# A second expert by half products in seven pairs of token tiles, with a fused sum and ReLU

## The chip, the cores and the metric

The kernel runs on one core of one Trainium2 chip. The metric is the time of one execution on the device, in microseconds. Three runs of the kernel before gave 377.02, 377.45 and 377.55 us; the median is 377.45. The profiled execution took 377.47 us, and the span from its first to its last instruction is 375.8 us. TensorE had its full clock throughout.

## The reference

Two layers follow each other. The first is attention over 4 batches, 8 heads, 768 positions of 64 values. Heads 0, 2 and 6 ("retrieval heads") see every earlier position; the other five see the first 4 positions ("sinks") and a window of the last 64. The second is a mixture of four experts, of which every token uses all four:

```python
a = softmax(where(mask, q @ k.T / 8, -1e9))
x = (a @ v) as 3072 tokens x 512
p = domain_probs / (domain_probs.sum(-1, keepdims=True) + 1e-9)
for e in range(4):
    h = maximum(x @ w1[e], 0.0)        # 512 -> 1024
    out += p[:, e:e + 1] * (h @ w2[e]) # 1024 -> 512
```

As p is not negative, it may be multiplied into x ahead of the first layer of an expert instead of into its result; the kernel does so for all but the first four token tiles.

## The kernel before, in words

**Tiles and stages.** The tokens are 24 tiles of 128. Attention works on eight units of three tiles (half a batch each). The first four tiles go through the experts plainly (`plain_steps`). The other twenty go two by two, as ten pairs (`pair_steps`, here counted from 0). A pair has two layers. In layer 1 each expert's hidden values are computed into `hA`, which is cut into blocks: `A11` and `A21` (the first half of the hidden values, for the first and the second tile), `A12` and `A22` (the second half), and a fifth. In layer 2 all four experts are multiplied by `w2` at once.

**Half products.** A product of 2 x 2 blocks is computed with seven block products instead of eight, after Strassen and Winograd, at the price of sums of blocks. Layer 2 does this in every pair: `second_sum`, `third_sum` and `fourth_sum` build S2 to S4 out of S1 (`first_sum`), and seven products (`product`, line 1290) accumulate in two PSUM banks x and y, in the order x y x y x y x. Between them ScalarE copies a bank to `s` (`keep`) and VectorE adds bank and copy into the output `o` (`add`, line 1313): after the second product out of y, after the fifth out of x, after the sixth out of y. In layer 1 expert 3 (`EW[0]`) is done so in every pair, and expert 2 (`EW[1]`) in the last `LAST = 3` pairs (`two(nt0)`); the other experts use `plain_layer1` (line 1154: eight matmuls of 256 columns a step). `winograd_layer1` has seven steps of eight matmuls of 128 columns (line 1183). They alternate between two banks of `pO`, with one bank of `pA` for the second step; each is followed by a copy on ScalarE (line 1193), or by a sum on VectorE out of PSUM (line 1199) with a ReLU in place behind it (line 1205), or, the last, by a ReLU on ScalarE.

**What VectorE prepares.** `scale_inputs(nt0, e)` (line 1112) multiplies the tokens of a pair by expert e's probabilities. `scaled_sums(e)` (line 1126 and two differences at 967) builds the block sums of an expert's inputs, and `first_weight_sums(e)` those of its `w1`, once. The sums for expert 2 are computed in the sixth and seventh pairs, into room that attention no longer needs (`room_for_more_sums`).

**The order.** All engines' instructions are in an order written out by hand; every engine works through its own queue in that order. A pair's layer 1 is a list of rows (`order`, lines 1250 and 1266): each names the steps to take from the generators n (plain), a and b (half products of experts 3 and 2) and then an operation, mostly for VectorE. A pair also prepares the next one: during and after its fifth and sixth product the inputs of experts 3 and 0 (and 2, if the next pair has two experts by half products: `ahead`) are scaled, and `scaled_sums` of expert 3 follows. Attention is put between these steps by a plan: each step reports its TensorE time times a share (0.5 in layer 1, 1.57 in layer 2), and while this sum is ahead of the plan of the current attention unit, one attention step is put in. An attention step is some scores (line 659), an exponent on ScalarE (677), a mask on VectorE (681), values (713, 785) and a normalisation (803, 808, 813 or 738 to 742); a unit begins by moving keys (273, 289).

**Keys and sinks.** The retrieval keys have two buffers `kR[0]` and `kR[1]`, by the parity of the batch; the values of the sinks that batches 1 to 3 need lie in `v_sinks`. POOL sets one key buffer to zero at line 1441, after the first attention unit, ahead of the loads of a later one. SP's queue carries the load of a pair's probabilities (`load_probs`, line 1089), the output's stores (1320) and the attention's transposes by DMA (262, 747).

Of the kernel before, what the change touches and what calls it, by code (L numbers as in the profile page):

```python
# [9 lines left out]

# [1 line left out]
FP16 = mybir.dt.float16  # L12
# [6 lines left out]
def kernel(  # L19
# [92 lines left out]

    EW = (E - 1, E - 2)
    KH, FN = DMP // 2, F // 2
    t1sb = pers.tile([P, 3, KH, FN], FP16, name="t1sb")
    hA = pers.tile([P, 5 * KT * P], FP16, name="hA")
    kR = []
    vR = []
    for i in range(2):
        kR.append(pers.tile([P, NCH, NR, 3, P], FP16, name=f"kR{i}"))  # L120
        vR.append(pers.tile([P, S // P, NR, D + 2], FP16, name=f"vR{i}"))
    kSf = pers.tile([P, NT * NSH * P], FP16, name="kS")
    vSf = pers.tile([P, NT * NSH * P], FP16, name="vS")

    kS = kSf.rearrange("p (c t s x) -> p c t s x", c=NCH, t=TC, s=NSH)
    vS = vSf.rearrange("p (c t s x) -> p c t s x", c=NCH, t=TC, s=NSH)

    def windows(x):

# [27 lines left out]


    kT = pers.tile([P, HP, P + CH], FP16, name="kT")
    v_sinks = pers.tile([NS, 1, NSH * P], FP16, name="v_sinks")  # L160

# [5 lines left out]
    def half(u):  # L167
        return slice(u * D, (u + 1) * D)
# [7 lines left out]

    def key_tile(b, c, h, t):

        i = b % 2
        if RETR[h]:  # L180
            return kR[i][:, t // 3, RH.index(h), t % 3, :]
# [88 lines left out]
    def keys_to_rows(b, c):  # L270

        for n, hps in ((slice(0, 2), slice(0, 2)), (slice(2, 3), slice(3, 4))):
            nc.vector.tensor_copy(
                out=kR[b % 2][half(0), c, n, :, :].rearrange("p n t x -> p n (t x)"),
                in_=kT[half(0), hps, P : P + CH],
            )

# [84 lines left out]
    def zero(eng, t):  # L362
        fill(eng, t.rearrange("p a b x -> p (a b x)"), 0.0)
# [53 lines left out]
    make_identity(nc, ident32)  # L417
    one_values(nc.vector, 0)
    load_v(0, 0, [0])
    zero(nc.vector, kR[0][:, 0, :, :, :])  # L420
    zero(nc.vector, kS[:, 0, :, :, :])
    nc.vector.tensor_copy(out=ident16, in_=ident32)

# [67 lines left out]
    load_v(0, 0, [2, 1, 3, 4, 6, 5, 7])  # L491
    load_w1(0, 0, F)
    load_w2(0)
    zero(gp, kR[0][:, 1, :, :, :])
# [44 lines left out]
    def attention(b, c):  # L539
# [8 lines left out]
        def transposes(hp):  # L548
            for x, is_k in ((q32 if first else qt16, 0), (k32 if first else k16, 1)):
                if first or hp > 1:  # L550
                    ps = bank()
                else:
                    ps = pV.tile([P, 512], FP32, name="pV", bufs=2)
                for j in range(3):
                    o = ps[:, j * P : (j + 1) * P]
                    if first:
                        nc.tensor.transpose(o, x[:, j, 2 * hp : 2 * hp + 2, :], ident32)
                        continue
                    for u in range(2):
# [12 lines left out]
                for u in range(2):  # L572
                    h = 2 * hp + u
                    r = slice(u * D, (u + 1) * D)
                    if RETR[h]:
                        nc.vector.tensor_copy(  # L576
                            out=rows_in_order(
                                kR[i][r, c, RH.index(h), :, :].rearrange(
                                    "r t x -> r (t x)"
                                )  # L580
                            ),
                            in_=cols(ps[r, :]),
                        )
                        continue
                    n = SH.index(h)
                    x_in, x_out = ps[r, 0:CH], kS[r, c, :, n, R0:P]
                    if first:
                        x_in = x_in.rearrange("r (t x) -> r t x", x=TK)
                    else:
                        x_in = x_in.rearrange("r (j t p) -> r j t p", j=3, t=TC)  # L590
                        x_out = x_out.rearrange("r t (p j) -> r j t p", j=3)
                    nc.vector.tensor_copy(out=x_out, in_=x_in)
                    sinks = kS[r, c, :, n, 0:NS]
                    if c == 0:
                        src = ps[r, 0:NS]
# [354 lines left out]

    hA16 = hA
    blocks = hA.rearrange("p (b k x) -> p b k x", b=5, k=KT)
    A11, A21, A12, A22, S1 = (blocks[:, n, :, :] for n in range(5))
    S2, S3, S4 = A11, A21, A12

    def whole_b(k, n, e, ft):
        return w2sb[:, e * FTP + k * HT + ft, n * HN : (n + 1) * HN]
# [20 lines left out]
        c = e * DMP + j * KH  # L978
        return w1sb[:, c : c + KH, k * FN : (k + 1) * FN]

    t1 = {(EW[0], n): t1sb[:, n, :, :] for n in range(3)}
# [10 lines left out]
    def room_for_more_sums():  # L992

        x = kR[0].rearrange("p c n t x -> p (c n t x)")
        y = att.tile([P, KH * FN], FP16, name="t1", tag="k_rows", bufs=1)
        for n in range(3):
            z = x[:, n * KH * FN : (n + 1) * KH * FN] if n < 2 else y
            t1[EW[1], n] = z.rearrange("p (c f) -> p c f", c=KH)
        x = att.tile([P, DMP * PC], FP16, name="xs1", tag="q16", bufs=1)
        own_room[EW[1]] = x.rearrange("p (c x) -> p c x", c=DMP)  # L1000

    own_room = {}

    def last_weight_sum(e):

# [126 lines left out]
    def first_sum(e, n=1):  # L1132
        k = slice(e * HT, (e + n) * HT)
        nc.vector.tensor_tensor(
            out=S1[:, k, :], in0=A21[:, k, :], in1=A22[:, k, :], op=ALU.add
        )


    PSHARE = 1.57

    LAST = 3

    def two(nt0):
        return nt0 >= pairs[-LAST]
# [1 line left out]
    def pair_steps(nt0, nxt):  # L1146
# [29 lines left out]
        def winograd_layer1(e, x, y):  # L1176
# [18 lines left out]
            def block(n):  # L1195
                return blocks[:, n, e * HT : (e + 1) * HT, :]

            def add(n, ps, b):
                nc.vector.tensor_tensor(  # L1199
                    out=block(b),  # L1200
                    in0=ps.rearrange("p (f x) -> p f x", f=HT),
                    in1=kept[n].rearrange("p (f x) -> p f x", f=HT),
                    op=ALU.add,
                )
                nc.vector.tensor_scalar(
                    out=block(b), in0=block(b), scalar1=0.0, scalar2=None, op0=ALU.max
                )

            def t(n):
# [29 lines left out]

        a, b = (winograd_layer1(e, *y) for e, y in zip(EW, (banks, banks[::-1])))  # L1240

        more, last_more = [], None
        if nt0 == pairs[-LAST - 2]:
            room_for_more_sums()
            more = first_weight_sums(EW[1])
        elif nt0 == pairs[-LAST - 1]:
            last_more = first_weight_sums(EW[1])[3]
        if not two(nt0):
            n = itertools.chain(*(plain_layer1(e) for e in range(E - 1)))
            order = (  # L1250
# [8 lines left out]
                ((n, a), lambda: first_sum(0, 2)),  # L1259
                ((n,), None),  # L1260
                ((n, n), lambda: first_sum(2, 2)),
                ((), lambda: scale_inputs(nxt, 1) if two(nxt) else None),
            )
        else:
            n = itertools.chain(plain_layer1(0), plain_layer1(1))
            order = (
                ((a, a, n), None),
                ((a, a, n), lambda: load_probs(nxt) if nxt else None),
                ((a, a, n), None),
                ((n,), lambda: scaled_sums(EW[1])),  # L1270
                ((a, b, n), None),
                ((b, b, n), lambda: first_sum(0)),
# [61 lines left out]

        last = nxt is None
        ahead = nxt and two(nxt)
        half = KT // 2 * mm_ns(HN), PSHARE
        yield from product(x, A11, b(0, 0), True)
        keep(0, x)
# [207 lines left out]
```

The softmax here doesn't subtract the row's maximum and nothing guards it: scores larger than these inputs give would overflow.

## Time and profile before

| | |
|---|---|
| median of three runs | 377.45 us |
| span of the profiled execution | 375.8 us |
| TensorE busy | 367.5 us (98%), 4128 matmuls |
| VectorE busy | 282.7 us (75%) |
| ScalarE busy | 227.8 us (61%) |
| plain layer 1, line 1154 | 864 matmuls of 256 columns |
| half products of layer 1, line 1183 | 728 matmuls of 128 columns |
| sums out of PSUM, line 1199 | 39, 26 of them at a mean of 687 ns |
| ReLUs in place, line 1205 | 39, mean 298 ns |
| scalings, line 1112, 1024 elements | 28, mean 1216 ns |

A matmul's duration in the trace includes its way through the array, and matmuls overlap; what one costs in a stream is the distance from its start to the next one's. "DVE" is VectorE, "ACT" ScalarE, "PE" TensorE and "PEld" its loading of weights. In a timeline a line is: start, duration, engine, line of the kernel, operation, what it writes and reads, shape, count of merged instructions, and in brackets the idle time before it and what ended it. VectorE's durations also overlap a little: for its pace, too, look at the starts. The ten pairs begin at about 88.1, 118.6, 149.3, 178.0, 209.5, 238.3, 267.8, 296.3, 321.7 and 347.2 us of the span; attention's last matmuls are in pair 6.

### The profile page before, as it was taken

The page shows a single profiled execution, that of the slowest core. Times are in us where ns is not written, and L with a number is a line of the kernel's source. Part 1 is how long each engine was busy: PE and PEld are TensorE (multiplying, and loading weights), DVE is VectorE, ACT ScalarE, POOL GpSimd, SP SyncE. Part 2 cuts the span into 40 slices and gives each one's busy share as a digit, 9 for nine tenths or more (in the row PEclk, how much of TensorE's full clock was granted, in tenths as well). Part 3 has the DMA queues.
Part 4 walks back from the last instruction along what each step waited for, and adds up shares of the span by engine and source line. Part 5 has one row for each costly group of instructions (what it writes and reads, how often), then busy time and mean ns, then how long its engine had stood idle before and what let it go on. Part 6 is the DMA issues. An engine that isn't in the chain of part 4 may idle for free.

```text
span 375.8 us, 10137 instructions
## 1 busy us (share of the span) xinstructions
PE 367.5 (98%) x4128; PEld 310.2 (83%) x4128; DVE 282.7 (75%) x620; ACT 227.8 (61%) x475; POOL 113.7 (30%) x155
## 2 busy tenths in 40 slices
PE   8889999999999999999999999999999999999996
PEld 4745466668998988999989898998899998999996
DVE  7774768697888679878758858967778868769572
ACT  3863478547785785765676955784777361450630
POOL 8934573882058038115601650320000000000000
PEclk9999999999999999999999999999999999999999
DMA  9999999999699599977904991951220300300101
GB/s 164 155 201 206 196 187 191 181 207 105 97 109 144 106 96 120 152 116 58 207 10 59 170 157 21 127 127 14 69 72 2 107 9 0 114 2 6 54 2 56
DMA packets 124771, 39.24 MB, mean 104 GB/s; under 512 B 113728, under 2 KB 118404, under 8 KB 124724
## 3 DMA queue, kind: packets, MB, share of 16 engines
q0 software_dynamic: 86848, 19.01, 59.1%
q1 hardware_dynamic: 36276, 19.18, 21.9%
q8 instruction: 32, 0.52, 0.6%
q10 hardware_dynamic: 1600, 0.39, 0.5%
q14 instruction: 15, 0.12, 0.1%
HBM read 44.89 MB, written 6.34 MB: 136 GB/s over the span
## 4 chain that ended last, share of the span: by engine, by line
PE 87%; DMA 7%; POOL 3%; DVE 2%; issue 0%; POOLq 0%
PE pO L1290 31%; PE pA L1154 25%; PE pO L1183 9%; DMA w2sb<-in_moe_w_dram 7%; PE pO L1048 6%; PE pA L659 5%; PE pA L1027 5%; PE pV L713 2%; PE pV L785 2%; PE pA L1183 2%; POOL vS L309 1%; POOL vR L303 1%; DVE xs L1112 1%; PE pA L1380 0%; POOL early L453 0%
## 5 line engine op out<-in xcount | busy, mean ns | idle before, releaser
L1290 PEld LDWEIGHTS <-hA 128*128 128x128 f16 x1104 | 104.9, 98 | 12.2
L1154 PE MATMUL pA<-xs,w1sb 128*128 128x256 f16 x864 | 109.3, 272 | 0.0
L1154 PEld LDWEIGHTS <-w1sb 128*128 128x128 f16 x864 | 80.7, 98 | 8.5
L1163 ACT ACTIVATE hA<-pA 128x512 f16<-128x512 f32 x108 | 64.4, 598 | 35.1 <-PE pA L1154 32.9
L1290 PE MATMUL pO<-w2sb,hA 128*128 128x256 f16 x640 | 76.7, 272 | 0.0
L677 ACT ACTIVATE es<-pA 128x384 f16<-128x384 f32 (+2 forms) x122 | 59.2, 511 | 27.1 <-PE pA L659 23.3
L305 POOL DMA_DIRECT2D vS<-in_v_dram x30 | 29.6, 989 | 111.7 <-PE pV L785 110.5
L1290 PE MATMUL pO<-tsb,hA 128*128 128x256 f16 x464 | 56.7, 272 | 0.0
L1112 DVE TENSOR_TENSOR xs<-xT,pB 128x1024 f16<-128x1024 f16 (+1 forms) x52 | 49.4, 969 | 1.2 <-DMA out_dram<-o 1.2
L967 DVE TENSOR_TENSOR hA<-hA 128x1024 f16<-128x1024 f16 x60 | 39.6, 684 | 0.4
L1040 ACT ACTIVATE hA<-pA 128x384 f16<-128x384 f32 (+1 forms) x64 | 22.2, 385 | 19.8 <-PE pA L1027 19.6
L1027 PE MATMUL pA<-xT,w1sb 128*128 128x384 f16 (+1 forms) x256 | 30.9, 273 | 1.3 <-DVE xT L766 0.8
L1048 PE MATMUL pO<-w2sb,hA 128*128 128x512 f16 x128 | 30.7, 379 | 0.3 <-DMA w2sb<-in_moe_w_dram 0.3
L1310 ACT COPY s<-pO 128x256 f32<-128x256 f32 x31 | 11.5, 372 | 27.7 <-PE pO L1290 21.9
L1027 PEld LDWEIGHTS <-w1sb 128*128 128x128 f16 x256 | 19.3, 98 | 10.2 <-issue 1.9
L808 DVE TENSOR_TENSOR xT<-pV,rc 64x384 f16<-64x384 f32 x37 | 20.5, 555 | 9.1 <-ACT rc L813 6.6
L1183 PEld LDWEIGHTS <-w1sb 128*128 128x128 f16 x416 | 26.3, 98 | 1.1 <-issue 0.2
L803 ACT ACTIVATE rc<-pV,eps 64x384 f32<-64x384 f32 x37 | 21.3, 576 | 6.5 <-PE pV L785 5.9
L1199 DVE TENSOR_TENSOR hA<-pO,s 128x512 f16<-128x512 f32 x26 | 17.9, 687 | 9.3 <-PE pO L1183 6.7
L681 DVE TENSOR_TENSOR es<-es,mS 128x384 f16<-128x384 f16 (+1 forms) x40 | 13.7, 343 | 13.4 <-ACT es L677 13.4
L659 PE MATMUL pA<-qT,kR 128*128 128x384 f16 (+2 forms) x120 | 22.9, 278 | 0.6 <-DVE kR L576 0.6
L1193 ACT COPY s<-pO 128x512 f32<-128x512 f32 x39 | 22.5, 585 | 1.4 <-PE pO L1183 1.2
(144 smaller groups left out, 498.2 us busy)
## 6 DMA issues: line engine op xcount, KB each, us to landing
pB<-p_rows SPq DMA_DIRECT2D x10, 512.0 KB
out_dram<-o SPq DMA_DIRECT2D x19, 256.0 KB
w1sb<-in_moe_w_dram POOLq DMA_DIRECT2D x8, 512.0 KB, 9.3
w2sb<-in_moe_w_dram POOLq DMA_DIRECT2D x4, 1024.0 KB, 12.5
vS<-in_v_dram POOLq DMA_DIRECT2D x30, 112.0 KB, 4.2
k_rows<-in_k_dram POOLq DMA_DIRECT2D x18, 128.0 KB, 5.6
q<-in_q_dram POOLq DMA_DIRECT2D x18, 128.0 KB, 6.4
vR<-in_v_dram POOLq DMA_DIRECT2D x24, 48.0 KB, 5.8
```

What stands on the lines that cost most here:

```text
L305: gp.dma_start(out=t[:, :, own_v(h)], in_=windows_of(v, b, h, c))
L659: nc.tensor.matmul(out=ps[:, o : o + nq], lhsT=key_tile(b, c, h, t), rhs=qTs[b, c][:, hp, q0 : q0 + nq], start=(n == 0 or not first), stop ...
L677: nc.scalar.activation(out=es[:, 0:cols], in_=ps[:, 0:cols], func=AF.Exp, scale=SC)
L967: nc.vector.tensor_tensor(out=out, in0=a, in1=b, op=ALU.subtract)
L1027: nc.tensor.matmul(out=pss[ft][:, 0:cols_n], lhsT=w1sb[:, e * DMP + ct, ft * P : (ft + 1) * P], rhs=x[:, ct, :], start=(n == 0), stop=(n = ...
L1048: nc.tensor.matmul(out=ps_o, lhsT=hs[:, ft, j * P : (j + 1) * P], rhs=w2sb[:, e * FTP + ft, :], start=(ft == 0), stop=(ft == FTP - 1),)
L1112: nc.vector.tensor_tensor(out=o, in0=xin, in1=pb.to_broadcast([P, DMP, n, P]), op=ALU.mult)
L1154: nc.tensor.matmul(out=ps[:, f * PC : (f + 1) * PC], lhsT=w1sb[:, e * DMP + ct, (f0 + f) * P : (f0 + f + 1) * P], rhs=xs[:, ct, :], start= ...
L1163: nc.scalar.activation(out=blocks[:, b0 : b0 + 2, k0 : k0 + 2, :].rearrange("p t f x -> p f t x"), in_=ps.rearrange("p (f t x) -> p f t x" ...
L1183: nc.tensor.matmul(out=ps[:, f * P : (f + 1) * P], lhsT=w[:, ct, f * P : (f + 1) * P], rhs=a[:, ct, :], start=(first and f == 0 and ct == ...
L1193: nc.scalar.copy(out=kept[n], in_=ps)
L1290: nc.tensor.matmul(out=ps, lhsT=a[:, k, :], rhs=b(k), start=(first and k == 0), stop=(k == KT - 1), skip_group_check=not first,)
```

## The change

- `LAST` goes from 3 to 7: expert 2 uses half products in pairs 3 to 9 instead of 7 to 9. Its sums of weights get a place of their own in `t1sb`, and are computed in pair 2: three in layer 1, the last at the pair's end.
- Sum and ReLU after a half product are one instruction, `TENSOR_ADD_SAT`, which gives max(min(in0 + in1, LARGEST), 0).
- One key buffer `kR` takes the place of two, and the second one's setting to zero is left out. `v_sinks` is the eighth tile of `vSf`, which batches 1 to 3 don't use.
- `first_sum` works in place: S1 is where A21 was, and S3 gets the fifth block.
- In pairs with two experts by half products, the scaled inputs of expert 2 take expert 1's old place, and those of expert 1 the first half of S3's block. Expert 1's are computed in the pair's own layer 1, after its first row, no longer in the pair before.

```diff
-    t1sb = pers.tile([P, 3, KH, FN], FP16, name="t1sb")
+    t1sb = pers.tile([P, 2, 3, KH, FN], FP16, name="t1sb")
-        kR.append(pers.tile([P, NCH, NR, 3, P], FP16, name=f"kR{i}"))
+    kR = pers.tile([P, NCH, NR, 3, P], FP16, name="kR")
+    v_sinks = vSf[0:NS, WT * NSH * P : (WT + 1) * NSH * P]
...
-    A11, A21, A12, A22, S1 = (blocks[:, n, :, :] for n in range(5))
-    S2, S3, S4 = A11, A21, A12
+    A11, S1, A12, A22, S3 = (blocks[:, n, :, :] for n in range(5))
+    S2, S4 = A11, A12
...
+    def room_for_two():
+        n = DMP * PC
+        own_room[EW[1]] = xs_of[0][:, n : 2 * n].rearrange("p (c x) -> p c x", c=DMP)
+        x = hA[:, 4 * KT * P : 4 * KT * P + n]
+        own_room[1] = x.rearrange("p (c x) -> p c x", c=DMP)
...
-            out=S1[:, k, :], in0=A21[:, k, :], in1=A22[:, k, :], op=ALU.add
+            out=S1[:, k, :], in0=S1[:, k, :], in1=A22[:, k, :], op=ALU.add
...
-    LAST = 3
+    LAST = 7
...
-                nc.vector.tensor_tensor(
+                nc.vector._custom_dve(
+                    TENSOR_ADD_SAT,
                     out=block(b),
                     in0=ps.rearrange("p (f x) -> p f x", f=HT),
                     in1=kept[n].rearrange("p (f x) -> p f x", f=HT),
-                    op=ALU.add,
-                )
-                nc.vector.tensor_scalar(
-                    out=block(b), in0=block(b), scalar1=0.0, scalar2=None, op0=ALU.max
+                    s0=LARGEST,
+                    s1=0.0,
                 )
...
-        if nt0 == pairs[-LAST - 2]:
-            room_for_more_sums()
+        if nt0 == pairs[-LAST - 1]:
             more = first_weight_sums(EW[1])
-        elif nt0 == pairs[-LAST - 1]:
-            last_more = first_weight_sums(EW[1])[3]
...
-                ((), lambda: scale_inputs(nxt, 1) if two(nxt) else None),
...
+                ((a, a, n), lambda: scale_inputs(nt0, 1)),
                 ((a, a, n), None),
                 ((a, a, n), lambda: load_probs(nxt) if nxt else None),
-                ((a, a, n), None),
...
-        if ahead and two(nt0):
-            scale_inputs(nxt, 1)
...
-        if last_more is not None:
-            last_more()
+        if more:
+            more[3]()
...
-    zero(gp, kR[1].rearrange("p c n t x -> p (c n) t x"))
```

More of the change, by code (lines that the diff above doesn't have):

```diff
@@ L7 @@
 from concourse.act_sets import SETS
+from concourse.dve_ops import TENSOR_ADD_SAT
 from concourse._compat import with_exitstack
@@ L114 @@
     KH, FN = DMP // 2, F // 2
-    t1sb = pers.tile([P, 3, KH, FN], FP16, name="t1sb")
+    t1sb = pers.tile([P, 2, 3, KH, FN], FP16, name="t1sb")
     hA = pers.tile([P, 5 * KT * P], FP16, name="hA")
-    kR = []
+    kR = pers.tile([P, NCH, NR, 3, P], FP16, name="kR")
     vR = []
     for i in range(2):
-        kR.append(pers.tile([P, NCH, NR, 3, P], FP16, name=f"kR{i}"))
         vR.append(pers.tile([P, S // P, NR, D + 2], FP16, name=f"vR{i}"))
@@ L126 @@
     vS = vSf.rearrange("p (c t s x) -> p c t s x", c=NCH, t=TC, s=NSH)
+    v_sinks = vSf[0:NS, WT * NSH * P : (WT + 1) * NSH * P]
+    v_sinks = v_sinks.rearrange("p (t x) -> p t x", t=1)
     def windows(x):
@@ L159 @@
     kT = pers.tile([P, HP, P + CH], FP16, name="kT")
-    v_sinks = pers.tile([NS, 1, NSH * P], FP16, name="v_sinks")
     x_pair = pers.tile([P, 3, P], FP16, name="x_pair")
@@ L177, in key_tile @@
     def key_tile(b, c, h, t):
-        i = b % 2
         if RETR[h]:
-            return kR[i][:, t // 3, RH.index(h), t % 3, :]
+            return kR[:, t // 3, RH.index(h), t % 3, :]
         if b:
@@ L273, in keys_to_rows @@
             nc.vector.tensor_copy(
-                out=kR[b % 2][half(0), c, n, :, :].rearrange("p n t x -> p n (t x)"),
+                out=kR[half(0), c, n, :, :].rearrange("p n t x -> p n (t x)"),
                 in_=kT[half(0), hps, P : P + CH],
@@ L419 @@
     load_v(0, 0, [0])
-    zero(nc.vector, kR[0][:, 0, :, :, :])
+    zero(nc.vector, kR[:, 0, :, :, :])
     zero(nc.vector, kS[:, 0, :, :, :])
@@ L493 @@
     load_w2(0)
-    zero(gp, kR[0][:, 1, :, :, :])
+    zero(gp, kR[:, 1, :, :, :])
     zero(gp, kS[:, 1, :, :, :])
@@ L577, in transposes @@
                             out=rows_in_order(
-                                kR[i][r, c, RH.index(h), :, :].rearrange(
+                                kR[r, c, RH.index(h), :, :].rearrange(
                                     "r t x -> r (t x)"
@@ L979, in w1_part @@
         return w1sb[:, c : c + KH, k * FN : (k + 1) * FN]
-    t1 = {(EW[0], n): t1sb[:, n, :, :] for n in range(3)}
+    t1 = {(e, n): t1sb[:, i, n, :, :] for i, e in enumerate(EW) for n in range(3)}
     def first_weight_sums(e):
@@ L990, in first_weight_sums @@
         ]
[L992 to L1000, printed above, removed]
-    own_room = {}
+    own_room = {}
+    def room_for_two():
[3 more added lines that the diff above has]
+        own_room[1] = x.rearrange("p (c x) -> p c x", c=DMP)
     def last_weight_sum(e):
@@ L1134, in first_sum @@
         nc.vector.tensor_tensor(
-            out=S1[:, k, :], in0=A21[:, k, :], in1=A22[:, k, :], op=ALU.add
+            out=S1[:, k, :], in0=S1[:, k, :], in1=A22[:, k, :], op=ALU.add
         )
+    LARGEST = 3.4028234663852886e38
     PSHARE = 1.57
-    LAST = 3
+    LAST = 7
     def two(nt0):
@@ L1240, in pair_steps @@
         a, b = (winograd_layer1(e, *y) for e, y in zip(EW, (banks, banks[::-1])))
-        more, last_more = [], None
-        if nt0 == pairs[-LAST - 2]:
-            room_for_more_sums()
+        more = []
+        if nt0 == pairs[-LAST - 1]:
             more = first_weight_sums(EW[1])
-        elif nt0 == pairs[-LAST - 1]:
-            last_more = first_weight_sums(EW[1])[3]
         if not two(nt0):
@@ L1336, in pair_steps @@
         ahead = nxt and two(nxt)
+        if ahead and not two(nt0):
+            room_for_two()
         half = KT // 2 * mm_ns(HN), PSHARE
```

## The prediction

> **What bounds the kernel now.** I read the engines' shares first, then TensorE's timeline around a pair, then the windows by layer, then VectorE's timeline at the seams between pairs. The reference span is the profiled execution's 375.8 us (that execution took 377.47 us; the three timed runs have a median of 377.45), so a change of the span is carried over one to one.
>
> ```profile
> PE 367.5 (98%) x4128; PEld 310.2 (83%) x4128; DVE 282.7 (75%) x620; ACT 227.8 (61%) x475; POOL 113.7 (30%) x155
> ...
> PE 87%; DMA 7%; POOL 3%; DVE 2%; issue 0%; POOLq 0%
> ```
>
> TensorE carries the chain that ended last. A busy PE need not be a full PE, so look at starts in its timeline (start, duration, line, count):
>
> ```profile
> 298.04 1.06 PE L1183 MATMUL pO<-kS,t1sb 128*128 128x128 f16 x16
> 298.93 1.04 PE L1154 MATMUL pA<-xs,w1sb 128*128 128x256 f16 x8
> ...
> 300.70 1.91 PE L1154 MATMUL pA<-xs,w1sb 128*128 128x256 f16 x16
> 302.44 0.61 PE L1183 MATMUL pO<-xs,t1sb 128*128 128x128 f16 x8
> ```
>
> 16 half-product matmuls take 298.93 - 298.04 = 0.89 us, 55.6 ns each; 16 plain ones 302.44 - 300.70 = 1.74 us, 109 ns each. Nothing stands between them: from 88 us on PE runs without gaps, but for some 0.7 us in all. So the kernel is worth what PE's matmuls cost plus any wait that gets in. The windows show which engine could make one (columns: stretch, length, then busy us and count of PE, PEld, DVE, ACT, POOL; first and second layer of the fifth pair, then of the eighth):
>
> ```profile
> 209.50:223.30 13.80, 13.80 (x166) 12.70 (x163) 9.12 (x19) 10.92 (x21) 9.63 (x12) 1.00 1.70 177
> 223.30:238.30 15.00, 15.00 (x191) 13.49 (x189) 12.89 (x36) 8.48 (x18) 2.00 (x2) 1.00 0.62 56
> ...
> 296.30:309.50 13.20, 13.20 (x176) 12.48 (x176) 8.99 (x21) 8.37 (x16) 0.00 (x0) 1.00 0.25 83
> 309.50:321.70 12.20, 12.20 (x116) 10.94 (x113) 10.60 (x22) 1.97 (x5) 0.00 (x0) 1.00 0.01 1
> ```
>
> VectorE is at 86% in a second layer where attention runs too (12.89 of 15.00), and at 87% in one without it.
>
> **What the Trainium skill says.** "TensorE: Matmul & The Clock Gate", section Back-to-back issue gap, gives about 81 ns a matmul for streams of 128 columns with weight loads. At that price 56 half-product matmuls (4.5 us) would cost more than the 32 plain ones. This trace has 55.6 ns, and decides. "VectorE: DVE Perf Modes", The perf-mode tier table, holds a tensor_tensor with a PSUM operand at 1x and a 16-bit one in SBUF at 2x; the trace agrees (512 elements from PSUM 687 ns, 1024 in SBUF 684). "DVE: opcode table, instruction layouts, handler registers and perf-mode slots", section 7, gives a two-source op its 2x only with 16-bit operands; the fused op reads fp32 from PSUM, so I price it as the add it replaces. "PSUM — Partial Sum Buffer", Engine vs sequencer instructions, calls the ScalarE and VectorE queues strict FIFO. The seams below show instructions in the order of the code, and my sum rests on that.
>
> **The change, part by part.**
>
> *Half products for expert 2 in pairs 3 to 6 (counted from 0; the last three have them already).* Removed per pair: 32 x 109 ns = 3.49 us. Added: 56 x 55.6 = 3.11. PE gains 0.37, in four pairs 1.5 us. ScalarE swaps four ReLUs of 598 ns for three copies of 585 and one ReLU of 595: nothing.
>
> *VectorE's load.* A converted pair adds the input sums (281 + 283 + 284 ns), a later difference (292), three sums out of PSUM (3 x 687), and splits two first sums of 686 into four of 422: +3.5 us. Fusion drops expert 3's three ReLUs of 298: net +2.6 in each of four pairs, -0.9 in each of the first three, -1.8 in each of the last three, +2.5 us over the kernel. By mean load that fits; only the order decides.
>
> *Scalings.* There are still four a pair. But converted pairs need experts 3, 0 and 2 scaled in the second layer before; now only 0 and 3 are there, and 3 stands after the sum that the next pair waits for. Expert 1's goes to the first layer. So a scaling (1.2 us) enters VectorE's queue ahead of the sums at L1313. Those free PSUM: the seventh product writes the bank that the first of them reads; the next pair's first half product, which in a converted pair comes at once, writes the bank that the second reads. The seam of today's seventh pair, which has this order, shows it:
>
> ```profile
> 295.81 0.41 DVE L1313 TENSOR_TENSOR o<-pO,s 128x256 f32<-128x256 f32 x1
> ...
> 296.27 0.61 PE L1183 MATMUL pO<-xs,w1sb 128*128 128x128 f16 x8
> ```
>
> The sum ends at 296.22, PE goes on at 296.27; the product before ended 0.16 us earlier. That is without attention. Now the seam after pair 4, with attention, as it is before:
>
> ```profile
> 233.58 0.68 DVE L967 TENSOR_TENSOR hA<-hA 128x1024 f16<-128x1024 f16 x1
> 234.18 0.35 DVE L681 TENSOR_TENSOR es<-es,mS 128x384 f16<-128x384 f16 x1
> 234.45 0.15 DVE L738 TENSOR_SCALAR rs<-pV 128x6 f32<-128x6 f32 x1
> ...
> 235.60 0.42 DVE L1313 TENSOR_TENSOR o<-pO,s 128x256 f32<-128x256 f32 x1
> 235.94 1.28 DVE L1112 TENSOR_TENSOR xs<-xT,pB 128x512 f16<-128x512 f16 x2
> 237.14 0.54 DVE L808 TENSOR_TENSOR xT<-pV,rc 64x384 f16<-64x384 f32 x1
> 237.61 0.40 DVE L1313 TENSOR_TENSOR o<-pO,s 128x256 f32<-128x256 f32 x1
> ```
>
> No idle time. Start to start a scaling in two pieces takes 237.14 - 235.94 = 1.2. Put expert 3's at 234.45: the first sum moves to 236.8 and ends at 237.2; the seventh product, which starts at 236.37, waits 0.85. Then the scaling of expert 0 (1.2), L808 (0.47), the input sums (0.75): the second sum ends at 239.95. The seventh product would end at 239.2 with its attention step, so the next pair waits 0.75. Together 1.6 us.
>
> The seam after pair 2:
>
> ```profile
> 174.56 0.42 DVE L1313 TENSOR_TENSOR o<-pO,s 128x256 f32<-128x256 f32 x1 [0.87 <-PE pO L1290]
> ...
> 176.74 0.42 DVE L1313 TENSOR_TENSOR o<-pO,s 128x256 f32<-128x256 f32 x1
> 177.08 1.22 DVE L1112 TENSOR_TENSOR xs<-xT,pB 128x1024 f16<-128x1024 f16 x1
> 178.33 0.56 DVE L808 TENSOR_TENSOR xT<-pV,rc 64x384 f16<-64x384 f32 x1
> 178.90 0.89 DVE L273 COPY kR<-kT 64x768 f16<-64x768 f16 x2
> ```
>
> Here 0.87 idle takes in the scaling, and the sum that frees PSUM ends at 177.85, in time (0.1 at most). But then come expert 2's scaling, L808, the keys of L273, and the last weight sum (684), now at this very place: VectorE reaches the first half-product sum at 180.9, ends expert 1's scaling at 182.7 and the difference that the sixth half product needs at 183.0. PE is there at about 182.05: 0.95. After pair 3 the sums are in time, but ScalarE holds two exponent steps until 211.05, so the copy that frees the third half product's bank ends near 211.65 against 211.3: 0.3. After pair 5 VectorE idles 0.88 before the sums: 0. Inside the first layers a copy must be back in 1.3 us (half product and plain step; 2.2 before) and takes 0.25 + 0.59: 0.2 for rare bursts. Sum: 1.6 + 1.05 + 0.3 + 0.2 = 3.2 us. Bounds: nothing, if every attention step falls in a kinder place, to 4.6, if pairs 5 and 6 lose like pair 4.
>
> *Later pairs.* Their second layers lose expert 1's scaling: the 0.16 at 296 goes.
>
> *Weight sums* (3 x 684 plus the last) move from pairs 5 and 6 to pair 2; the three stand in its first layer, 12.4 of 15.0 us busy before: nothing beyond the seam above. *One key buffer:* L273 at 178.90 now overwrites keys that the scores of the attention unit two before read, over 30 us earlier for one half, some 20 for the other: no wait. A 1.1 us memset leaves POOL, whose next loads are used from some 75 us on: nothing either way. *Sinks in vS:* the same transfers, behind values long finished. *Sum in place:* the same instruction; the block it frees lends its first half to expert 1's scaled input, read out 3.5 us before. *Probabilities' load:* on SP it waits for expert 1's scaling; queued behind are the attention's transposes and the output's stores, which wait a microsecond at most, and its data are used a layer later. *Fused op:* from 0.62 start to start (as the add) to 0.99 (as both); I take 0.62.
>
> Sum: -1.5 - 0.15 + 3.2 = +1.55: 377.45 + 1.55 = 379.0 us.
>
> **Rivals.**
> 1. *The seams hold, PE's gain stays* (0.31). For it: attention steps are placed by PE time spent, a converted pair spends less, and a step of 0.2 to 0.6 us shifted by half a product changes a seam; before, no seam lost over 0.3 us. Against: VectorE is full from 228.7 to 240 and a shift by one step doesn't empty it. 377.45 - 1.65 + 0.3 = 376.1. It decides once the waits stay under 0.9 us.
> 2. *Half the waits* (0.19): one of the two large seams holds; 377.5, no change to be told.
> 3. *ScalarE becomes the bound in first layers* (0.07): ten to twelve of 15 us busy with attention; each of four pairs loses another 0.3: 380.2.
> 4. *The fused op is slow* (0.05): 0.3 us more each, six in a converted pair, about half of it on PE: 382 at worst.
>
> Main case, the two seams lose most of what I worked out: 0.38, its own range 378.2 to 379.9.
>
> **How the numbers follow.** A difference under 0.2% (0.75 us) is about what a measurement of this kernel can't tell from none. Faster is rival 1: 0.31. Same is rival 2: 0.19. Slower is the main case with rivals 3 and 4: 0.50. The range reaches from a little under rival 1 (375.9, all but the last existing gaps gone) to 380.6.
>
> **What would show it.** PE's matmul count rises by 4 x 24 = 96; L1183's by 224. VectorE's waits at L1313 vanish in pairs 2 to 5, and PE shows waits for L1313 at L1290 (seventh product of pair 4) and L1183, and at L1183 for L967 early in pair 3. Fused sums at about 690 ns, no L1205. Wrong if those waits are absent, if the fused op lasts over 0.8 us, or if PE waits for keys or loads.

## The result, and the profile after

The changed kernel takes 383.15 us (median; 383.04 to 383.39), the kernel before 377.45: a ratio of 1.0154, with an interval of 1.0137 to 1.0172. I had said 379.0, and 375.9 to 380.6. The sign is right and the size is not: +5.7 instead of +1.55.

The span of the profiled execution grew from 375.8 to 381.7 us, by 5.9. The first lines of the page (busy time, share and instructions of each engine; then the chain that ended last) say where it did not go:

```profile
PE 368.1 (96%) x4224; PEld 310.8 (81%) x4224; DVE 283.2 (74%) x617; ACT 227.6 (60%) x475; POOL 111.5 (29%) x154
...
PE 81%; DVE 12%; ACT 4%; issue 2%; DVEq 0%; ACTq 0%
```

TensorE has 96 matmuls more, as worked out, and VectorE is about as busy as before in the sum (283.2 us after 282.7). What changed is the chain: VectorE holds 12% of it instead of 2%, ScalarE 4% where it had no share. The list of TensorE's waits (what waited, for whom; us in total, times, longest) names the places; none of the six was in the list before:

```profile
PE pV L786 <- DVE xT L809: 1.2, 1, 1.2
PE pO L1184 <- DVE o L1310: 1.1, 2, 0.9
PE pO L1184 <- DVE xs L969: 1.1, 2, 0.9
PE pO L1184 <- ACT s L1194: 1.0, 2, 0.5
PE pO L1287 <- DVE o L1310: 0.7, 1, 0.7
PE pO L1287 <- DVE hA L1201: 0.2, 1, 0.2
```

(Lines have moved: half products are now at 1184, plain ones at 1155, layer 2 at 1287, its sum at 1310, scalings at 1111, input sums at 1125, differences at 969, the fused sum at 1201, the copies at 1194, attention's normalisation at 804, 809 and 814.) They add up to 5.3 us. That is too little: the list counts a wait from the end that the trace gives a matmul, and a matmul of 128 columns lasts 219 ns there, though starts lie 55.6 ns apart. So each wait comes out 0.16 us too short, and the smallest are missing. I therefore took another count: the distance from each matmul's start to the next one's, less what its columns cost in a stream; what is over is a loss. By pair (from the start of a pair's first matmul of layer 1 to that of the next pair's, for pair 9 to the end of the span; TensorE's clock is full in all):

| pair | before: us | lost | after: us | lost |
|---|---|---|---|---|
| 2 | 28.62 | 0 | 29.02 | 0.41 |
| 3 | 31.53 | 0.26 | 33.26 | 2.35 |
| 4 | 28.80 | 0 | 30.75 | 2.49 |
| 5 | 29.54 | 0 | 30.55 | 1.16 |
| 6 | 28.44 | 0.16 | 28.98 | 1.07 |
| 7 to 9 | 79.5 | 0 | 79.5 | 0 |

Lost in pairs 2 to 6: 7.48 instead of 0.42, so 7.06 more. What pairs 3 to 6 take without the losses fell from 117.89 to 116.47, by 1.42. The stretch ahead of pair 0, where loads and the first attention unit lie, took 0.29 more (87.8 to 88.6 over all the profiles here, whatever was changed). 7.06 - 1.42 + 0.29 = 5.9.

Four of the places follow, each by its engine's own timeline. First VectorE at the seam after pair 4, the one that the prediction worked through:

```profile
237.11 1.29 DVE L1111 TENSOR_TENSOR xs<-xT,pB 128x512 f16<-128x512 f16 x2
...
239.21 0.41 DVE L1310 TENSOR_TENSOR o<-pO,s 128x256 f32<-128x256 f32 x1
239.54 1.28 DVE L1111 TENSOR_TENSOR xs<-xT,pB 128x512 f16<-128x512 f16 x2
...
242.21 0.41 DVE L1310 TENSOR_TENSOR o<-pO,s 128x256 f32<-128x256 f32 x1
```

In the lines left out there is no hole either. Both sums at L1310 now stand behind expert 3's scaling of 1.2 us (237.11), which followed them before; the second also stands behind the input sums. And TensorE in the same stretch:

```profile
239.68 1.03 PE L1287 MATMUL pO<-tsb,hA 128*128 128x256 f16 x8 [0.67 <-DVE o L1310]
...
242.67 0.55 PE L1184 MATMUL pO<-xs,w1sb 128*128 128x128 f16 x7 [0.90 <-DVE o L1310]
```

The first sum ends at 239.62, and the seventh product goes on at 239.68; the second ends at 242.62, and the next pair's half product starts at 242.67. By the distance of starts the two lose 0.83 and 1.07 us.

Second, a seam that the prediction called harmless on VectorE, after pair 3 (VectorE, then TensorE):

```profile
209.68 0.42 DVE L1310 TENSOR_TENSOR o<-pO,s 128x256 f32<-128x256 f32 x1
210.01 1.22 DVE L1111 TENSOR_TENSOR xs<-xT,pB 128x1024 f16<-128x1024 f16 x1
211.14 0.54 DVE L809 TENSOR_TENSOR xT<-pV,rc 64x384 f16<-64x384 f32 x1
```

```profile
211.74 0.34 PE L786 MATMUL pV<-es,vS 128*128 128x48 f16 x7 [1.17 <-DVE xT L809]
```

The sum of layer 2 is indeed in time. But behind it comes expert 2's scaling, new in this place, and behind that L809, which reads a bank of `pV`. There are two of these, and the values of the next attention step need one: 1.33 us lost, where 0.26 was lost before.

Third, ScalarE in pair 6:

```profile
284.94 0.58 ACT L804 ACTIVATE rc<-pV,eps 64x384 f32<-64x384 f32 x1
285.55 0.52 ACT L814 ACTIVATE rc<-rc 64x384 f32<-64x384 f32 x1
286.10 0.59 ACT L1194 COPY s<-pO 128x512 f32<-128x512 f32 x1
```

The copy that frees the half product's bank stands behind the logarithm and the exponent of an attention step, and ends at 286.69, 1.75 us after the first of the three began; TensorE, which has waited 0.51 us, goes on at 286.73. Pair 5 has the same at 245.91 to 247.65. Fourth, early in pair 3 (VectorE, then TensorE):

```profile
178.52 1.22 DVE L1111 TENSOR_TENSOR xs<-xT,pB 128x1024 f16<-128x1024 f16 x1
...
182.18 1.22 DVE L1111 TENSOR_TENSOR hA<-xT,pB 128x1024 f16<-128x1024 f16 x1
183.31 0.28 DVE L969 TENSOR_TENSOR xs<-xs,kS 128x256 f16<-128x256 f16 x1
```

```profile
183.66 0.62 PE L1184 MATMUL pO<-xs,w1sb 128*128 128x128 f16 x8 [0.86 <-DVE xs L969]
```

As worked out, the difference at L969 stands behind expert 2's scaling, the last weight sum (180.87) and expert 1's scaling, and TensorE waits 0.86 for it until 183.66; by the distance of starts 1.02 is lost.

### The profile page after: what moved, and what is told of

It reads as the page before. It is cut to its first block, busy times and chain, and to the rows that moved or that the text cites. A ratio compares the mean times of both kernels' runs of the same rounds, so it can differ in the third digit from the quotient of the medians.

```text
span 381.7 us, 10324 instructions
## 1 busy us (share of the span) xinstructions
PE 368.1 (96%) x4224; PEld 310.8 (81%) x4224; DVE 283.2 (74%) x617; ACT 227.6 (60%) x475; POOL 111.5 (29%) x154
## 4 chain that ended last, share of the span: by engine, by line
PE 81%; DVE 12%; ACT 4%; issue 2%; DVEq 0%; ACTq 0%
PE pO L1287 25%; PE pA L1155 19%; PE pO L1184 10%; PE pA L1026 7%; PE pO L1047 7%; PE pA L660 4%; DVE xs L1111 2%; PE pA L1184 2%; PE pV L714 2%; ACT rc L804 2%; PE pV L786 1%; DVE xT L809 1%; DVE hA L969 1%; PE pO L430 1%; DVE es L682 1%
## 5 line engine op out<-in xcount | busy, mean ns | idle before, releaser
L1164 ACT ACTIVATE hA<-pA 128x512 f16<-128x512 f32 x92 | 55.0, 598 | 37.0 <-PE pA L1155 35.1
L1155 PEld LDWEIGHTS <-w1sb 128*128 128x128 f16 x736 | 68.7, 98 | 6.9
L1155 PE MATMUL pA<-xs,w1sb 128*128 128x256 f16 x512 | 64.6, 273 | 0.0
L1111 DVE TENSOR_TENSOR xs<-xT,pB 128x1024 f16<-128x1024 f16 (+1 forms) x43 | 40.8, 969 | 0.0
L969 DVE TENSOR_TENSOR hA<-hA 128x1024 f16<-128x1024 f16 x60 | 39.7, 685 | 0.4
L1184 PEld LDWEIGHTS <-w1sb 128*128 128x128 f16 x544 | 33.8, 98 | 5.5 <-issue 3.0
L1184 PE MATMUL pO<-xs,w1sb 128*128 128x128 f16 x408 | 30.6, 219 | 3.3 <-DVE o L1310 1.1
L1201 DVE CUSTOM_DVE_ANT_0 hA<-pO,s 128x512 f16<-128x512 f32 x34 | 23.1, 689 | 12.2 <-ACT s L1194 6.5
L1194 ACT COPY s<-pO 128x512 f32<-128x512 f32 x51 | 29.4, 588 | 4.0 <-PE pO L1184 2.7
L1155 PE MATMUL pA<-hA,w1sb 128*128 128x256 f16 x224 | 29.0, 273 | 0.0
L1026 PEld LDWEIGHTS <-w1sb 128*128 128x128 f16 x256 | 19.4, 98 | 10.2 <-issue 1.9
L1184 PEld LDWEIGHTS <-t1sb 128*128 128x128 f16 x408 | 25.9, 98 | 1.1 <-issue 0.2
```

The source lines that it names most:

```text
L969: nc.vector.tensor_tensor(out=out, in0=a, in1=b, op=ALU.subtract)
L1026: nc.tensor.matmul(out=pss[ft][:, 0:cols_n], lhsT=w1sb[:, e * DMP + ct, ft * P : (ft + 1) * P], rhs=x[:, ct, :], start=(n == 0), stop=(n = ...
L1111: nc.vector.tensor_tensor(out=o, in0=xin, in1=pb.to_broadcast([P, DMP, n, P]), op=ALU.mult)
L1155: nc.tensor.matmul(out=ps[:, f * PC : (f + 1) * PC], lhsT=w1sb[:, e * DMP + ct, (f0 + f) * P : (f0 + f + 1) * P], rhs=xs[:, ct, :], start= ...
L1164: nc.scalar.activation(out=blocks[:, b0 : b0 + 2, k0 : k0 + 2, :].rearrange("p t f x -> p f t x"), in_=ps.rearrange("p (f t x) -> p f t x" ...
L1184: nc.tensor.matmul(out=ps[:, f * P : (f + 1) * P], lhsT=w[:, ct, f * P : (f + 1) * P], rhs=a[:, ct, :], start=(first and f == 0 and ct == ...
```

## The experiments

The theory: the matmuls gain what was said, and the loss is queueing. Over the whole kernel VectorE and ScalarE have hardly more to do than before, but in pairs with attention the instruction that TensorE needs stands behind one of 0.5 to 1.2 us that could as well stand behind it. Rivals: one of the other parts costs (fused op, one key buffer, sum in place); the mean load is too high, so that any order waits.

**All but the number of pairs.** Everything of the change stays, but only three pairs have two experts by half products:

```diff
-    LAST = 7
+    LAST = 3
```

> The changed kernel with only the number of pairs back at three. Theory (waits that VectorE's and ScalarE's queues make in pairs 3 to 6 cost 7 us, TensorE gains 1.4): all waits of these pairs go, and with them the gain: 377.2 us, at most 0.3 off the kernel before, with the 0.16 us wait at the seam of pair 6 gone. Rival (the other parts cost time themselves: the fused instruction, one key buffer, the sum in place, expert 1's scaling in the pair's own first layer): 379 us or more.

Measured: 377.66 us, 1.0007 times the kernel before (0.9999 to 1.0016). In its trace pairs 2 to 6 lose 0.26 us together, as before the change, and the 0.16 ahead of pair 7 is gone. So key buffer, sinks, the sum in place and the fused op cost nothing that shows in the trace, and by the interval at most 0.6 us; the rest of the 5.7 us comes with the four more pairs. (The weight sums lie in pair 6 here, ahead of the three pairs; that the three of the first layer cost nothing in pair 2 either is seen two experiments below, where that pair loses nothing. The last one stands in the queue of early pair 3.)

**Sum and ReLU apart again**, with seven pairs:

```diff
-                nc.vector._custom_dve(
-                    TENSOR_ADD_SAT,
...
+                nc.vector.tensor_tensor(
...
+                    op=ALU.add,
+                )
+                nc.vector.tensor_scalar(
+                    out=block(b), in0=block(b), scalar1=0.0, scalar2=None, op0=ALU.max
```

> The changed kernel with sum and ReLU as two instructions again. Theory (VectorE's queue is full where TensorE waits, and the fused instruction takes 0.62 us start to start as the sum alone does): each converted pair gets six more instructions of 0.26 us, a part of it on waits: 384 to 385.5 us. Rival (the fused instruction is what slows the queue): faster than the changed kernel, 381 to 382 us.

Measured: 384.24 us (1.0185; 1.017 to 1.02), 1.1 more than the changed kernel. The groups of instructions give the price (the changed kernel's line, then this kernel's two):

```profile
L1201 DVE CUSTOM_DVE_ANT_0 hA<-pO,s 128x512 f16<-128x512 f32 x34 | 23.1, 689 | 12.2 <-ACT s L1194 6.5
```

```profile
L1201 DVE TENSOR_TENSOR hA<-pO,s 128x512 f16<-128x512 f32 x34 | 23.4, 687 | 8.2 <-ACT s L1194 4.7 <-PE pO L1184 3.3
L1207 DVE TENSOR_SCALAR hA<-hA 128x512 f16<-128x512 f16 x51 | 15.3, 301 | 1.8
```

689 ns for the fused sum, 687 for the plain one with 301 behind it. The extra loss is where VectorE's queue was already late: early pair 3 loses 1.37 instead of 1.02, pair 4 0.68 instead of 0.37, pair 6's second layer 0.68 instead of 0.35. Fusion helps, and it isn't the cause of the loss.

**Another order at the seams.** Expert 3's scaling behind the sum after the fifth product, input sums and expert 0's scaling behind the sum after the sixth, expert 2's in its own first layer:

```diff
-            x, S3, b(0, 1), False, lambda: scale_inputs(nxt, EW[0]) if ahead else None
+            x, S3, b(0, 1), False
...
-            scale_inputs(nxt, 0)
+            scale_inputs(nxt, EW[0] if ahead else 0)
...
-            scale_inputs(nxt, EW[1] if ahead else EW[0])
+        if ahead:
+            scaled_sums(EW[0])
+            scale_inputs(nxt, 0)
...
-                ((a, a, n), None),
+                ((a, a, n), lambda: scale_inputs(nt0, EW[1])),
```

> The changed kernel with VectorE's queue reordered at the seams: ahead of a pair with two experts by half products, expert 3's inputs are scaled behind the sum after the fifth product, the input sums and expert 0's scaling behind the sum after the sixth, and expert 2's scaling in the pair's own first layer behind its second row. No work is left out. Theory (the place of these scalings makes the waits at the seams): the waits after pairs 2, 3 and 4 (0.4, 1.3, 0.8 and 1.1 us) and the one early in pair 3 (1.0) go down to 1 us together, those of ScalarE's copies in the first layers stay: 379.5 us. Rival (attention's load on VectorE and ScalarE is too high for any order): waits only move, 382.5 to 383.5.

Measured: 381.94 us (1.0124; 1.0109 to 1.014). The seams after pairs 2 and 4 lose nothing now (0.41 and 1.90 in the changed kernel), and the values after pair 3 0.98 instead of 1.33. But pair 5 waits 0.82 us at its first plain step for a scaling, pair 3 0.22, and pair 6 loses 1.59 instead of 1.07. Early pair 3 still loses 1.07: there expert 0's scaling now stands where expert 2's stood. Of 2.66 us gained at the seams only 1.04 are left, and the time lies nearer to the rival's 382.5 than to the 379.5 that I expected.

**No attention step between two half products that follow each other** (the steps are handed on as one until a plain one comes):

```diff
-            for x in steps:
-                yield next(x)
+            held = 0.0
+            for x, then in zip(steps, (*steps[1:], None)):
+                ns, share = next(x)
+                if x is not n and then is not n and then is not None:
+                    held += ns
+                    continue
+                yield held + ns, share
+                held = 0.0
```

> The changed kernel, but no attention step is put between two half products that stand side by side in a row; it comes behind the second. Theory for the waits in the first layers of pairs 5 and 6 (the copy after the fourth half product stands on ScalarE behind a logarithm and an exponent of attention, 1.1 us): the two waits of 0.7 us go: 381.7 us. Rival (the copy waits for VectorE to free its room): no change, 383.1.

Measured: 382.43 us (1.0133; 1.0116 to 1.015). Pair 5's loss of 0.69 is gone (1.16 to 0.46); pair 6's 0.67 stays, as there logarithm and exponent come between a plain step and a half product.

**Expert 2's scaling left out**, so that only this one instruction is missing:

```diff
-            scale_inputs(nxt, EW[1] if ahead else EW[0])
+            if not ahead:
+                scale_inputs(nxt, EW[0])
```

> The changed kernel without the scaling of expert 2's inputs ahead of the seven pairs (that part of the computation is left out: seven VectorE instructions of 1.2 us). Theory (this scaling stands in front of what TensorE waits for after the seams): the wait for the difference early in pair 3 (1.0 us) and the one of the values' matmuls for L809 after pair 3 (1.3) go, as does the one early in pair 4 (0.4); those in front of it in the queue stay (0.4, 0.8 and 1.1 at the seams after pairs 2 and 4), and the copies' on ScalarE (0.7 twice): 380.5 us. Rival (VectorE's load as a whole): all VectorE's waits shrink alike, and 379 us or less.

Measured: 381.3 us (one execution, as in the other two runs below that leave work out). Pair 3 loses 0.35 instead of 2.35: both its large waits, 1.02 early and 1.33 at the values, hung on an instruction of 1.2 us. Pairs 5 and 6 lose what they lost, and the sums at L1310 are as they were. Pair 4's 0.37 for the difference stayed, against the theory, and ahead of it the third half product now loses 0.52 instead of 0.22:

```profile
211.83 1.05 PE L1184 MATMUL pO<-kS,t1sb 128*128 128x128 f16 x16 [0.36 <-ACT s L1194]
...
214.59 0.62 PE L1184 MATMUL pO<-xs,w1sb 128*128 128x128 f16 x8 [0.21 <-DVE xs L969]
```

VectorE's timeline tells why the second wait stayed:

```profile
211.81 0.69 DVE L1201 CUSTOM_DVE_ANT_0 hA<-pA,s 128x512 f16<-128x512 f32 x1 [1.60 <-ACT s L1194]
```

VectorE stands idle for 1.60 us until ScalarE's copy is done; only then come this fused sum, L809, expert 1's scaling and the difference. So this wait begins with ScalarE, not with expert 2's scaling.

**Masks of attention left out** in units 4 to 7 (0.22 to 0.35 us of VectorE each; nothing of the change is touched):

```diff
-                for m, mo, o0, o1 in () if first else masks:
+                for m, mo, o0, o1 in () if first or g > 3 else masks:
```

> The changed kernel without the mask multiplications of attention units 4 to 7 (left out: 11 short VectorE instructions a unit, some 3.5 us each unit; all four units fall in pairs 2 to 6). Theory (attention's own VectorE work, packed into second layers, is the other half of the queue at the seams): the waits at the seams after pairs 3 and 4 (1.3, 0.8, 1.1) fall by more than half, the copies' waits on ScalarE (0.7 twice) stay: 380.5 us. Rival (the scalings' place alone makes the waits): less than 0.7 us gained, 382.5.

Measured: 381.66 us. The seam after pair 4 loses 0.14 instead of 1.90, the values after pair 3 0.78 instead of 1.33. Pairs 5 and 6 lose exactly what they lost (1.16 and 1.07). So the losses at the seams come from a full queue of VectorE, and those in pairs 5 and 6 don't hang on these masks. Of the 2.3 us less that these are, the span shows 1.8: the stretch from the last pair's start to the end, where nothing is lost in TensorE, took 29.10 us instead of 28.56.

**A better order by hand**, from what these showed: the third's and the fourth's edits, expert 0's scaling ahead of the input sums, experts 2 and 1 scaled after the second and third row of layer 1, the last weight sum in pair 3:

```diff
-                ((a, a, n), lambda: scale_inputs(nt0, 1)),
                 ((a, a, n), None),
-                ((a, a, n), lambda: load_probs(nxt) if nxt else None),
-                ((n,), lambda: scaled_sums(EW[1])),
+                ((a, a, n), lambda: scale_inputs(nt0, EW[1])),
+                ((a, a, n), last_scaling),
+                ((n,), after_sums),
```

> Nothing left out. As e3_order and e4_atom together, with three places changed again: expert 0's scaling stands before the input sums (pair 5's first plain step waited 0.8 us for it), expert 2's scaling comes behind the second row and expert 1's behind the third, and the last weight sum moves from the end of pair 2 into pair 3's first layer. Theory (each wait has its own instruction in front of it, and can be moved off): early in pair 3 1.0, in pair 4 0.4, in pair 5 0.8 and 0.7 go; left are some 1 us after pair 3 and 1.5 in the first layers: 378.7 us. Rival (the waits move elsewhere): 380.5 or more.

Measured: 381.97 us (1.0111; 1.0093 to 1.013), no better than the plainer edit, and a miss for the theory: I expected 378.7. Pairs 2 and 3 lose 0.98 instead of 2.76, but pairs 5 and 6 lose 4.58 instead of 2.23: two plain steps lose 0.76 each, waiting for expert 1's scaling, and a half product in pair 5 loses 1.02, waiting for a fused sum behind expert 2's. In none of the orders tried did 1.2 us of VectorE find a place that is free in every pair with attention; the rival is right that far.

**Four pairs instead of seven, and attention done earlier**, so that none of the four has any:

```diff
-    LAST = 7
+    LAST = 4
...
-    for a, n in zip(range(2, G), (0.72, 1.65, 2.95, 4.15, 5.4, 6.65)):
+    for a, n in zip(range(2, G), (0.72, 1.6, 2.7, 3.75, 4.8, 5.9)):
```

> As e7_order2 with four pairs (one more than before), and attention planned earlier so that it ends within pair 5: ends of units 3 to 7 at 1.6, 2.7, 3.75, 4.8 and 5.9 pairs instead of 1.65, 2.95, 4.15, 5.4 and 6.65. Theory (a pair without attention takes half products without waits and gains TensorE's 0.37 us): 376.9 to 377.2 us, if the denser attention costs pairs 1 to 5 nothing. Rival (denser attention makes waits there too): 378 or more.

Measured: 378.49 us (1.0027; 1.0018 to 1.0037). Pair 6, by half products and without attention, takes 25.47 us and loses nothing, like the last three. But pairs 1 to 3 lose 2.0 us instead of 0.46: attention is denser there. That is what the rival said.

**The same, with only the last three units earlier:**

```diff
-    for a, n in zip(range(2, G), (0.72, 1.6, 2.7, 3.75, 4.8, 5.9)):
+    for a, n in zip(range(2, G), (0.72, 1.65, 2.95, 3.95, 4.95, 5.95)):
```

> Half products for expert 2 in four pairs (6 to 9), the order of the run with LAST = 4, but the attention units 2, 3 and 4 end where they do in the changed kernel (0.72, 1.65, 2.95 pairs) and only units 5, 6 and 7 earlier (3.95, 4.95, 5.95), so that pair 6 is free of attention. Theory (waits come from VectorE's and ScalarE's queues where attention and a converted pair meet): pair 6 takes 25.5 us without a wait, pairs 1 to 3 lose at most 0.5 us together as in the kernel before, instead of 2.0 with the denser plan; pairs 4 and 5, now with more attention, lose up to 0.5. 376.6 to 377.4 us, ratio to the kernel before 0.998 to 1.0. Rival (any denser attention costs what pair 6 gains): 378.0 to 378.6.

Measured: 378.67 us (1.0019; 1.0009 to 1.003); what I hoped for didn't come. Pairs 3 and 5 lose 0.75 and 0.56 us (0.26 and 0 before), at the values' banks; these 1.05 us more are twice what pair 6 gains (0.37 of matmuls and the 0.16). Another 0.7 us lies at the end: from the end of the last sum to the end of the span it took 3.28 us here, 2.55 in the run before this one. Whether that belongs to this order or to this one profile is open.

**The exponent of the normalisation left out** in units 4 to 7 (0.52 us of ScalarE each), in the changed kernel:

```diff
-                nc.scalar.activation(out=rc[r, :], in_=rc[r, :], func=AF.Exp, scale=-1.0)
+                if g < 4:
+                  nc.scalar.activation(out=rc[r, :], in_=rc[r, :], func=AF.Exp, scale=-1.0)
```

> The changed kernel; left out is the second of two ScalarE steps of the normalisation (the exponent that turns minus the logarithm of the sum into its reciprocal) in attention units 4 to 7. Theory (the copies that free the half products' banks in pairs 5 and 6 stand behind logarithm and exponent in ScalarE's queue, 0.6 us each): the waits for L1194 of 0.53 and 0.51 us vanish, and pairs 5 and 6 lose at most 0.5 and 0.5 us instead of 1.16 and 1.07; the waits for VectorE in pairs 3 and 4 stay within 0.3 us. About 382.0 us. Rival (VectorE's lateness holds up the step ahead of the copy, and the copy is only the last in the row): pairs 5 and 6 lose what they lost, 382.9 to 383.4.

Measured: 380.55 us. Pair 5 loses 0.14 instead of 1.16, pair 6 0.47 instead of 1.07, pair 4's early losses (0.22 and 0.37) are gone; the waits for VectorE stay: 1.89 at pair 4's seam, and in pair 3 1.19 and 1.33. The same stretch of ScalarE's timeline in pair 6 (the copy is at L1195 in this kernel):

```profile
282.71 0.58 ACT L804 ACTIVATE rc<-pV,eps 64x384 f32<-64x384 f32 x1
283.32 0.59 ACT L1195 COPY s<-pO 128x512 f32<-128x512 f32 x1
```

The copy follows the logarithm directly, and the loss at this half product is 0.12 us instead of 0.67. So from pair 4 on the losses inside the first layers come from ScalarE's queue; in pair 4 one of them passes through VectorE, as seen above. Early pair 3 is VectorE's. Of the 2.8 us that the span is shorter, 2.16 are these losses; 0.63 is the stretch ahead of pair 0.

The losses of all together (us by pair, from the distance of starts; spans of the profiled executions; pair 1 loses 0.20 in each, but 0.80 with four pairs and attention earlier):

| kernel | 2 | 3 | 4 | 5 | 6 | sum | span |
|---|---|---|---|---|---|---|---|
| before | 0 | 0.26 | 0 | 0 | 0.16 | 0.42 | 375.8 |
| after | 0.41 | 2.35 | 2.49 | 1.16 | 1.07 | 7.48 | 381.7 |
| three pairs | 0 | 0.26 | 0 | 0 | 0 | 0.26 | 375.6 |
| sum and ReLU apart | 0.41 | 2.70 | 2.80 | 1.16 | 1.40 | 8.47 | 382.5 |
| another order | 0 | 2.27 | 0.60 | 1.98 | 1.59 | 6.44 | 380.3 |
| half products together | 0.40 | 2.37 | 2.49 | 0.46 | 1.07 | 6.79 | 380.7 |
| no scaling of expert 2 | 0.40 | 0.35 | 2.79 | 1.15 | 1.06 | 5.75 | 379.6 |
| no masks | 0.40 | 1.81 | 0.74 | 1.16 | 1.07 | 5.18 | 379.9 |
| better order | 0 | 0.98 | 0.68 | 2.50 | 2.08 | 6.24 | 380.3 |
| four pairs, attention earlier | 0.50 | 0.70 | 0 | 0 | 0 | 1.20 | 377.3 |
| four pairs, last units earlier | 0 | 0.75 | 0 | 0.56 | 0 | 1.31 | 377.0 |
| no exponent | 0.25 | 2.52 | 1.94 | 0.14 | 0.47 | 5.32 | 378.9 |

## Why the prediction was right in kind and wrong in size

- *TensorE's gain, 1.5 us:* 1.42 found. The 0.16 ahead of pair 7: gone in the run with three pairs, as said.
- *Seam after pair 4, 0.85 + 0.75:* 0.83 + 1.07. *Early pair 3, 0.95:* 1.02, and the difference at 183.31 where 183.0 was said. *After pair 2, at most 0.1:* 0.41; the sum ended at 178.60, not at 177.85. The pair began 0.3 later, and 0.87 of idle time doesn't take in a scaling of 1.2: the rest pushed both sums back by another 0.3.
- *After pair 3, 0.3, put down to a copy on ScalarE:* the copy came as said, behind logarithm and exponent, and cost pair 4's third half product 0.22. But the step as a whole failed. It found the sum of layer 2 in time and stopped there. What stood behind expert 2's scaling wasn't followed: L809 and the `pV` bank that it holds, 1.33 us. My own account of the same seam one pair earlier listed L809 behind that scaling, as a burden for what came later in VectorE's queue, never as the release of a bank.
- *First layers, "0.2 for rare bursts":* this is the term that was mis-sized most. Beside that 0.22, pair 4 lost 0.37, pair 5 0.69 and 0.22 (and 0.25 as its second layer began), pair 6 0.67, where nothing was lost before: 2.2 us in all. The step compared a copy's 0.84 us with the 1.3 that a bank has, and took attention's activations as rare. But a normalisation puts 0.58 and 0.52 back to back ahead of the copy, and 1.1 + 0.59 is over 1.3. Leaving the exponent out took away 0.54, 1.02 and 0.55 us in the three pairs (pair 4's 0.22 among them). That is rival 3, ScalarE in the first layers, at about twice its price, and beside the main case, not in its place. To count them as cases that exclude each other was a fault of the range: it ends at 380.6, while 379.0 with 2.0 us more from here and 1.0 more from after pair 3 (1.33 and 0.22, less the 0.3 said and the 0.26 lost there before) would have been 382.0.
- *Upper bound 4.6, "if pairs 5 and 6 lose like pair 4":* 7.06 was found, and not in that way: the seams after pairs 5 and 6 lose at most 0.05. Nor does the sum come out: two more pairs at 1.6 on top of 3.2 are 6.4.
- *Pair 6, second layer:* 0.35 at its start, for the last fused sum; not in the working. Sum and ReLU apart make it 0.68, so it is VectorE's queue.
- *Fused op, keys, sinks, sum in place, the first layer's weight sums, probabilities at nothing:* right within 0.6 us, by the run with three pairs (the weight sums by the one with another order).

"PSUM — Partial Sum Buffer", section Engine vs sequencer instructions, of the Trainium skill calls these queues strict FIFO. The timelines here agree: at the seam after pair 4 VectorE takes scaling, sum, scaling and sum in the order of the code (237.11, 239.21, 239.54, 242.21), none past another. So does the run that leaves an instruction out: without expert 2's scaling, 2.0 us of waits that stood behind it in pair 3 went too.

Mean loads would have told little. In pairs 3 to 6 VectorE was busy 91.1 of 118.3 us before (77%) and 96.1 of 123.5 after (78%), with all of the increase in pairs 3 and 4 (3.0 and 2.5 us); ScalarE went from 80.0 to 79.5 us, and yet 2.1 us of the losses in pairs 4 to 6 went with its exponent. Still open is what a copy queue without attention's activations ahead of it would be worth together with a better order at the seams; and four pairs with the plan of attention as it was weren't tried. No version here beats the kernel before.

## What to carry to other kernels

When an edit puts an instruction into a queue, follow every later instruction of that queue until the next idle time, and ask of each which buffer it frees; that the first is in time proves nothing for the second. When TensorE has less work between two uses of a buffer, work out anew how long the buffer has to come back, and compare that with the longest row of foreign instructions that can stand ahead of the release, not with the mean load. Causes that sit on different engines can add up, as they did here: their costs belong in one sum, not among the rivals.

## What the hardware showed beyond that

- A fused sum with clamping at both ends, 512 elements of fp32 from PSUM and SBUF to 16 bits, costs 689 ns, the sum alone 687, and its pace from start to start is 0.61 us.
- The tail of a profile, from the end of the last sum to the end of the span, differs with the same stores and without a matmul, a sum or an activation in it: about 2.55 us in ten of the twelve profiles here, 3.1 without the masks and 3.3 with four pairs and the last units earlier. With differences under 0.7 us, look at the tail first.
